# Order and issue of the last convolution step's loads in a fused state-space and feed-forward kernel

## The chip, the cores and the metric

The kernel runs on one core of a Trainium2 chip. The metric is the device time of one execution in microseconds (us). Several executions of a kernel are taken, and their median is compared. One more execution is recorded by the hardware profiler; its span, from the first to the last instruction, is what the profile's views are about. PE is the matrix engine, DVE the vector engine, ACT the scalar engine, POOL and SP the engines that here mainly issue DMAs.

## The reference, cut to what matters

For x of 2048 positions and D = 576 channels, with xn = layernorm(x), the kernel computes

```python
out = x + A(xn) + B(xn)
# A: a long convolution along the positions, one filter per channel
K = einsum("dn,dnl,dn->dl", C, exp(dt*A)**l, dt*B).real     # 576 filters of length 2048
A(u) = irfft(rfft(pad(u)) * rfft(pad(K)))[:2048] + u * Dskip
# B: a feed-forward layer, F = 4608
B(u) = silu(u @ w1) @ w2
```

All of it is in float32.

## The kernel before, in words

**The feed-forward part** is the main line of the program (`ffn`, L231). The positions are cut into 16 tiles j of 128; tiles 0 to 7 are half 0, tiles 8 to 15 half 1, and four tiles make a block. F is cut into 9 chunks c of 4 x 128. The loop runs over `(half, c, b)`, 36 blocks numbered from 0. A block has up products (`up`, L283: x by w1, then silu and a split into a high and a low part, gh and gl) and down products (`down`, L303: by w2, added to the tile's accumulator `acc` by DVE, L320). Products are taken in three passes over high and low parts. A block's steps are u0, d0, d1, d2, d3, u1, u2, u3: its four down products, and the four up products of the block behind it, t = 0 to 3. An up product is 14 matmuls on 512 columns, a down product 24 on 288. The last chunk, c = 8 of half 1, is blocks 34 and 35; its weights are asked for in block 32 (L382: `load_w1` 0, `load_w2` 0 and 1, `load_w1` 2, `load_w2` 2 and 3), and `pins["load"]` is the last load so far. For that chunk the loads with t = 2 and 3 go into the pool `yp` (L243, L268), which takes the place of the pool `kl` of the spectral part.

When half 0 is done, its accumulators are written to `dr0` in DRAM (L323) and the buffers go to half 1. The convolution is added to tiles 0 to 7 later: `dr0` is loaded again in pairs of tiles (`load_r0`, L733, tile `r0`, shown as `r` in the profile), the convolution is added, and the pair is stored to the output by POOL (`store`, L169, issue on L172). Tiles 8 to 15 get theirs in the accumulator, at the head of their last down product (L307 to L309). At the end of the program tiles 8 to 15 are stored by SP, POOL and ACT (L862 to L865).

**The convolution** is a side line (`side`, L805): a transform of the inputs, of the filters, and products of both, written to `d2` in DRAM (`spectral`, L675; 32 stores by POOL, L724). Its last step is `add_conv` (L783): for tile j it takes the tile `ys` (two DMAs of 288 KB on SP, `conv_load`, L776), does 8 small float32 matmuls with the fixed matrix s4 into two PSUM tiles `py` (L793; they show as 16 records, 64*32 rows by columns, 288 columns), and adds both to the destination by DVE (L799). A tile of `ys` takes rows from all 32 stores of d2. There are 8 buffers of ys, 4 of r0 and 3 of `pss`, from which py comes.

**What sets the order.** `weave` (L32) runs the side line between the steps of the main line: a side step with the number `at` is run as soon as `at * 288 <= i + 1`, where i + 1 counts the main line's steps. Block n has the counts 5 + 8n to 12 + 8n (u0 first), so block 32 has 261 to 268, block 33 269 to 276, block 34 277 to 284, and block 35, which has only d0 to d3, 285 to 288. Such a count is called a gate here. The framework then puts each engine's instructions in order itself, by a simulated timeline and by priority (L940: `schedule_with_timeline_sim=True`); an instruction traced earlier has the higher priority, `high_priority` raises it, and `behind(ins)` (L135) keeps what is traced inside it behind `ins` on the same engine. In `add_conv` the first of the matmuls stays behind the last feed-forward matmul traced so far, and the others are of high priority behind the first.

The last step is written out in `tail` (L729). With `tail_at = (0.895, 0.0045, 0.922, 0.005)` the loads are spread over gates from 258 to 273 (L743 to L747), and convolutions 0 to 7 (`last`, L737) over gates from 266 to 276. They are run sorted by these numbers, and `last(j)` first asks for the tile six further on, if that is tile 8 or later; `down` does the same for its own tiles (L308):

```python
        steps, at = [], tail_at[0]
        for j in range(8):
            for f in (conv_load, load_r0)[:2 - j % 2]:
                steps.append((at, f, j))
                at += tail_at[1]
        steps += [(tail_at[2] + j * tail_at[3], last, j) for j in range(8)]
```

Of the kernel before, what the change touches and what calls it, by code (L numbers as in the profile page):

```python
# [11 lines left out]
F32 = mybir.dt.float32  # L12
# [6 lines left out]
P = 128  # L19
# [4 lines left out]
NJ = 16  # L24
NKT = 4
HD = D // 2
# [16 lines left out]
def kernel(  # L43
# [89 lines left out]
    pins = {}  # L133

    def behind(ins):  # L135
        return tc.issue_after(ins) if ins is not None else nullcontext()
# [24 lines left out]
    def load_x(j, pool, tag, engines):  # L161

        t = pool.tile([P, 2, D], F32, tag=tag, name=f"{tag}{j}")
        for ps, v, eng in quarters(xv, engines):
            eng.dma_start(t[ps], v[:, j:j + 2])
        pairs[j] = t
        return t[:, 0, :], t[:, 1, :]

    def store(t, j, engines):  # L169

        for ps, v, eng in quarters(ov, engines):
            eng.dma_start(v[:, j:j + 2] if len(t.shape) > 2 else v[:, j], t[ps])  # L172
# [26 lines left out]
    def phase0(p0, js):  # L199
        j0 = js[0]  # L200
        xs = load_x(j0, accp, "acc", (nc.sync, nc.scalar) if j0 < 4 else (nc.sync,))
        acc.update(zip(js, xs))
        if j0:
            normed(p0, js, xs)
        else:
            for j, xj in zip(js, xs):
                normed(p0, (j,), (xj,))
# [23 lines left out]
    def ffn():  # L231
# [71 lines left out]
        def down(blk, jj):  # L303
            half, c, b = blk
            j = 8 * half + 4 * b + jj
            js = slice(jj * P, (jj + 1) * P)
            if half == 1 and c == NCH - 1:  # L307
                conv_load(j + AHEAD)  # L308
                add_conv(j, acc[j])  # L309
            for h in range(2):  # L310
                hs = slice(h * HD, (h + 1) * HD)
                po = ps2.tile([P, 512], F32, tag="ps2", name="po")
                n = 0
                for t in range(FT):
                    for g, w in ((0, 0), (0, 1), (1, 0)):
                        pins["pe"] = nc.tensor.matmul(po[:, :HD], G[blk, t][g][:, js], W2[half, c, t][w][:, hs],  # L316
                                                      start=n == 0, stop=n == 3 * FT - 1).ins
                        n += 1
                with tc.high_priority():
                    nc.vector.tensor_add(acc[j][:, hs], po[:, :HD], acc[j][:, hs])  # L320
            if half == 0 and c == NCH - 1:
                rows = slice(j * P, (j + 1) * P)
                nc.sync.dma_start(dr0[rows, :], acc[j])  # L323
                if j % 2:
                    acc[7 + j], acc[8 + j] = load_x(7 + j, accp, "acc", (nc.sync,))
# [398 lines left out]
            nc.gpsimd.dma_start(d2.rearrange("(p k) d -> k p d", k=32)[k], yo)  # L724
            yield 1 + (k + 1) / 32

    AHEAD = 6

    def tail():  # L729

        r0s = {}

        def load_r0(j):  # L733
            r0s[j] = yp.tile([P, 2, D], F32, tag="r0", name="r0", bufs=4)
            nc.sync.dma_start(r0s[j], dr0[j * P:(j + 2) * P, :].rearrange("(i p) d -> p i d", p=P))

        def last(j):  # L737
            conv_load(j + AHEAD, 8)
            add_conv(j, r0s[j - j % 2][:, j % 2, :])
            if j % 2:  # L740
                store(r0s[j - 1], j - 1, (nc.gpsimd,))

        steps, at = [], tail_at[0]  # L743
        for j in range(8):
            for f in (conv_load, load_r0)[:2 - j % 2]:
                steps.append((at, f, j))
                at += tail_at[1]  # L747
        steps += [(tail_at[2] + j * tail_at[3], last, j) for j in range(8)]
        for at, f, j in sorted(steps, key=lambda v: v[0]):
            yield at  # L750
            with behind(pins["load"]):
                f(j)

    yss = {}

# [17 lines left out]
                nc.tensor.matmul(dst, st, mv[:, hs], start=n == 0, stop=n == 3 * len(terms) - 1)  # L773
                n += 1

    def conv_load(j, first=0):  # L776
        if first <= j < NJ:
            yss[j] = yp.tile([P, 4, HD], F32, tag="ys", name="ys", bufs=AHEAD + 2)
            for h in range(2):
                nc.sync.dma_start(yss[j][64 * h:64 * h + 64],  # L780
                                  d2[j * 256:(j + 1) * 256, h * HD:(h + 1) * HD].rearrange("(q r) d -> r q d", q=4))

    def add_conv(j, dst):  # L783

        ys = yss.pop(j)
        py = [pss.tile([P, 512], F32, tag="pss", name="py") for _ in range(2)]
        first = pins["pe"]
        for n in range(8):
            q1, q2, h = n // 4, n // 2 % 2, 1 - n % 2
            o = 64 * q1 + 32 * q2  # L790
            rows = slice(64 * h, 64 * h + 64)
            with tc.high_priority() if n else nullcontext(), behind(first):
                mm = nc.tensor.matmul(py[h][o:o + 32, :HD], s4[rows], ys[rows, 2 * q2 + q1],  # L793
                                      start=True, stop=True, tile_position=(64 * h, o), skip_group_check=True)
            if n == 0:
                first = mm.ins
        for h in range(2):
            hs = slice(h * HD, (h + 1) * HD)
            nc.vector.tensor_add(dst[:, hs], py[h][:, :HD], dst[:, hs])  # L799

    def gate_of(i):

        return (FT + i * 2 * FT + 1) / (2 * NCH * 2 * 2 * FT)

    def side():  # L805
        nonlocal s4, kl, yp, pa, tail_at
        marks = (0.13, 0.597, 0.823)
        tail_at = (0.895, 0.0045, 0.922, 0.005)
        with tc.tile_pool(name="pa", bufs=4) as pa:
            for js in ((0, 1), (2, 3), (4, 5), (6, 7)):  # L810
                with behind(pins["xt3"] if js[0] > 2 else None):
                    phase0(pa, js)
                pins[f"xt{js[1]}"], pins[f"xt{js[1]}s"] = pins["xt_v"], pins["xt_s"]
                if js[0] == 2:
                    yield 0
            yield 0
        with tc.tile_pool(name="kf", bufs=1) as kfp:
            for n in ("f", "phi"):
                kf[n] = kfp.tile([P, D], F32, name=n + "T")
            with tc.tile_pool(name="nat", bufs=1) as nat, tc.tile_pool(name="pb", bufs=1) as pb:  # L820
                nt = natural(nat)
                def late(j):

                    xs = load_x(j, pb, "xj", (nc.sync,))
                    yield
                    with behind(pins["gl"]):
                        normed(pb, (j, j + 1), xs)
                    yield

                tiles = chain.from_iterable(late(j) for j in range(8, NJ, 2))  # L830
                for at, todo in ((0.0, nt), (0.0, tiles), (0.004, tiles), (0.005, tiles), (gate_of(0), nt), (0.026, tiles), (0.028, tiles), (0.036, tiles), (0.038, tiles), (gate_of(1), nt), (0.06, tiles), (gate_of(2), nt), (0.09, nt)):
                    yield at
                    with behind(pins["gl"] if at else None):
                        next(todo, None)
            with behind(pins["sd"]):
                nc.gpsimd.dma_start(f1, cf1)
            nc.sync.dma_start(vt, cv)
            with tc.tile_pool(name="up", bufs=1) as up:
                sp = spread(up)
                for n, at in enumerate(kgen()):  # L840
                    if n > 1:
                        next(sp, None)
                    yield marks[0] + at * (marks[1] - marks[0])
                for _ in sp:
                    pass
        s4p = ctx.enter_context(tc.tile_pool(name="s4p", bufs=1))
        s4 = s4p.tile([P, 32], F32, name="s4")
        nc.gpsimd.dma_start(s4, cs4)

        with tc.tile_pool(name="kl", bufs=2) as kl:  # L850
            for at in spectral():
                yield marks[1] + (at - 1) * (marks[2] - marks[1])
        yp = ctx.enter_context(tc.tile_pool(name="yp", bufs=3))
        yield from tail()

    sd = side()
    next(sd)
    fg = ffn()
# [85 lines left out]
```

## Time and profile before

| what | us |
|---|---|
| median of 3 executions | 1133.96 |
| lowest and highest of them | 1133.13, 1138.07 |
| the profiled execution | 1134.37 |
| its span | 1132.6 |
| PE busy in the span | 1108.6 |
| DVE busy | 916.8 |
| ACT busy | 709.3 |

The mean granted clock of PE is 0.997 of full speed. DMA moved 148.56 MB, 131 GB/s over the span. The busy time of an engine says how much of the span it worked, not whether it set the end; for that one reads the chain of work that ended last, the waits of the busiest engine, and the stretches in which it was idle. An issue on SP or POOL is a short entry in that engine's list; the transfer itself lands some microseconds later. In a list in order of time each line has the start, the length, the engine, the line of the kernel, the operation, the tile written and the tiles read, the shape and the count of merged instructions; in brackets stands how long the engine had been idle before, and what ended it.

### The profile page before, as it was taken

The page shows a single profiled execution, that of the slowest core. Times are in us where ns is not written, and L with a number is a line of the kernel's source. Part 1 is how long each engine was busy: PE and PEld are TensorE (multiplying, and loading weights), DVE is VectorE, ACT ScalarE, POOL GpSimd, SP SyncE. Part 2 cuts the span into 40 slices and gives each one's busy share as a digit, 9 for nine tenths or more (in the row PEclk, how much of TensorE's full clock was granted, in tenths as well). Part 3 has the DMA queues.
Part 4 walks back from the last instruction along what each step waited for, and adds up shares of the span by engine and source line. Part 5 has one row for each costly group of instructions (what it writes and reads, how often), then busy time and mean ns, then how long its engine had stood idle before and what let it go on. Part 6 is the DMA issues. An engine that isn't in the chain of part 4 may idle for free.

```text
span 1132.6 us, 22870 instructions
## 1 busy us (share of the span) xinstructions
PE 1108.6 (98%) x9144; PEld 998.8 (88%) x9144; DVE 916.8 (81%) x1545; ACT 709.3 (63%) x1229; POOL 73.0 (6%) x130
## 2 busy tenths in 40 slices
PE   6999999999999999999999999999999999999898
PEld 5988889898898898889989999999999999997776
DVE  6798799999999899999999737777778787773433
ACT  4565366677767676676766636787777787772211
POOL 1100100000000000011000000000000000001110
PEclk9999999999999999999999999999999999999999
DMA  9546431425252415265743263554555454426971
GB/s 277 152 121 168 122 83 60 107 81 128 71 116 84 115 60 129 70 152 168 193 143 93 67 165 115 150 154 134 160 152 159 127 158 141 132 89 170 248 179 56
DMA packets 174971, 148.56 MB, mean 131 GB/s; under 512 B 110944, under 2 KB 141680, under 8 KB 174736
## 3 DMA queue, kind: packets, MB, share of 16 engines
q1 hardware_dynamic: 164768, 112.07, 37.8%
q0 software_dynamic: 9712, 34.14, 9.4%
q8 instruction: 72, 1.18, 0.5%
q10 hardware_dynamic: 384, 0.89, 0.3%
q14 instruction: 35, 0.29, 0.1%
HBM read 102.53 MB, written 44.61 MB: 130 GB/s over the span
## 4 chain that ended last, share of the span: by engine, by line
PE 77%; DMA 7%; DVE 7%; issue 4%; SPq 2%; ACT 2%; POOL 0%; ACTq 0%; DVEq 0%; POOLq 0%
PE po L316 33%; PE ph L291 27%; DMA ys<-d 3%; PE kp L641 3%; PE ph L293 2%; PE ph L292 2%; PE pu L773 2%; PE pk L773 2%; PE pb L773 2%; PE z L656 2%; PE pu L154 1%; SPq L228 1%; DVE st L181 1%; DMA xj<-in_A_u_dram 1%; DVE gl L301 1%
## 5 line engine op out<-in xcount | busy, mean ns | idle before, releaser
L316 PE MATMUL po<-w2h,gh 128*128 128x288 f32 x1152 | 338.6, 298 | 1.0 <-ACT w2h L278 0.9
L316 PE MATMUL po<-w2l,gh 128*128 128x288 f32 x1152 | 339.0, 295 | 0.0
L316 PE MATMUL po<-w2h,gl 128*128 128x288 f32 x1152 | 337.1, 296 | 2.0 <-DVE gl L301 1.8
L316 PEld LDWEIGHTS po<-w2h,gh 128*128 128x128 f32 x1152 | 215.9, 188 | 11.6 <-issue 3.7
L316 PEld LDWEIGHTS po<-w2h,gl 128*128 128x128 f32 x1152 | 216.1, 188 | 4.8 <-DVE gl L301 2.8
L316 PEld LDWEIGHTS po<-w2l,gh 128*128 128x128 f32 x1152 | 217.0, 188 | 3.7
L299 ACT ACTIVATE gf<-ph 128x512 f32<-128x512 f32 (+1 forms) x148 | 86.5, 585 | 126.1 <-PE ph L293 109.3
L320 DVE TENSOR_TENSOR acc<-po,acc 128x288 f32<-128x288 f32 x288 | 127.1, 454 | 46.9 <-PE po L316 45.0
L291 PE MATMUL ph<-xh,w1h 128*128 128x512 f32 (+1 forms) x592 | 163.3, 391 | 1.4 <-ACT xh L124 0.7
L291 PE MATMUL ph<-xl,w1h 128*128 128x512 f32 (+1 forms) x592 | 162.9, 389 | 0.0
L291 PE MATMUL ph<-xh,w1l 128*128 128x512 f32 (+1 forms) x592 | 162.5, 387 | 0.3 <-DVE w1l L261 0.3
L301 DVE TENSOR_TENSOR gl<-gf,gh 128x512 fp32r<-128x512 f32 (+1 forms) x148 | 99.4, 674 | 39.8 <-ACT gh L300 39.0
L291 PEld LDWEIGHTS ph<-xl,w1h 128*128 128x128 f32 x592 | 109.5, 191 | 20.7
L291 PEld LDWEIGHTS ph<-xh,w1l 128*128 128x128 f32 x592 | 108.2, 189 | 21.0 <-DVE w1l L261 0.7
L291 PEld LDWEIGHTS ph<-xh,w1h 128*128 128x128 f32 x592 | 105.7, 190 | 20.3 <-issue 2.3
L300 ACT CAST gh<-gf 128x512 fp32r<-128x512 f32 (+1 forms) x148 | 89.8, 609 | 14.2 <-PE po L316 11.2
L278 ACT CAST w2h<-w2r 128x576 fp32r<-128x576 f32 x72 | 46.9, 672 | 44.8 <-PE po L316 27.9
L600 ACT ACTIVATE c<-th 128x1040 f32<-128x1040 f32 x36 | 38.7, 1074 | 49.3 <-DVE th L599 49.3
L598 ACT ACTIVATE c<-th,magic 128x1040 f32<-128x1040 f32 x36 | 42.0, 1168 | 33.2 <-DVE th L584 17.2
L261 DVE TENSOR_TENSOR w1l<-w1r,w1h 128x640 fp32r<-128x640 f32 x72 | 57.1, 822 | 0.2
L292 PE MATMUL ph<-x,w1h 128*128 128x512 f32 (+1 forms) x148 | 57.1, 386 | 0.0
L293 PE MATMUL ph<-x,w1l 128*128 128x512 f32 (+1 forms) x148 | 57.1, 386 | 0.0
(182 smaller groups left out, 1829.2 us busy)
## 6 DMA issues: line engine op xcount, KB each, us to landing
w2r<-in_B_w_dram SPq DMA_DIRECT2D x72, 288.0 KB, 3.3
w1r<-in_B_w_dram SPq DMA_DIRECT2D x35, 512.0 KB, 4.1
d1u<-u POOLq DMA_DIRECT2D x32, 288.0 KB, 2.7
d1k<-stage SPq DMA_DIRECT2D x18, 512.0 KB, 7.4
ur<-d1u SPq DMA_DIRECT2D x32, 288.0 KB, 4.1
kr<-d1k SPq DMA_DIRECT2D x32, 288.0 KB, 2.8
d<-yo POOLq DMA_DIRECT2D x32, 288.0 KB, 3.6
ys<-d SPq DMA_DIRECT2D x32, 288.0 KB, 12.4
```

Source lines behind the costliest of these rows:

```text
L261: pins["w1l"] = nc.vector.tensor_sub(l1, src, h1).ins
L278: pins["w2h"] = nc.scalar.copy(h2, r2).ins
L291: nc.tensor.matmul(ph, w[:, kt, :], v[:, kt, a:e], start=n + kt == 0, stop=False)
L292: nc.tensor.matmul(ph, h1[:, 4, :], x4[:, a:e], start=False, stop=False)
L293: pins["pe"] = nc.tensor.matmul(ph, l1[:, 4, :], x4[:, a:e], start=False, stop=True).ins
L299: nc.scalar.activation(gf, ph, AF.Silu)
L300: pins["gh"] = nc.scalar.copy(gh, gf).ins
L301: pins["gl"] = nc.vector.tensor_sub(gl, gf, gh).ins
L316: pins["pe"] = nc.tensor.matmul(po[:, :HD], G[blk, t][g][:, js], W2[half, c, t][w][:, hs], start=n == 0, stop=n == 3 * FT - 1).ins
L320: nc.vector.tensor_add(acc[j][:, hs], po[:, :HD], acc[j][:, hs])
L598: nc.scalar.activation(c65, th, AF.Identity, bias=magic)
L773: nc.tensor.matmul(dst, st, mv[:, hs], start=n == 0, stop=n == 3 * len(terms) - 1)
```

## The change

The six-ahead rule is gone. `conv_load` takes no tile any more; each call takes the next of a fixed order, 0 to 3, 8 to 11, 4 to 7, 12 to 15. At gate 263 the first eight loads are traced at once, with r0 pairs 0 and 2 among them, all behind `pins["load"]`, which by then is the last weight load of the last chunk. The other eight are asked for behind a convolution each, so each takes the buffer that this convolution has read. r0 pairs 4 and 6 are loaded behind convolutions 1 and 2. Convolutions 0 to 3 have the gates 269 to 272 and convolutions 4 to 7 the gates 278, 279, 280 and 282 (0.932 and 0.965 of 288 and 0.0036 apart). Convolutions 8 to 15 stay at the heads of their down products.

```diff
--- before.py
+++ after.py
@@ -305,8 +305,8 @@
             j = 8 * half + 4 * b + jj
             js = slice(jj * P, (jj + 1) * P)
             if half == 1 and c == NCH - 1:
-                conv_load(j + AHEAD)
                 add_conv(j, acc[j])
+                conv_load()
             for h in range(2):
                 hs = slice(h * HD, (h + 1) * HD)
                 po = ps2.tile([P, 512], F32, tag="ps2", name="po")
@@ -724,7 +724,8 @@
             nc.gpsimd.dma_start(d2.rearrange("(p k) d -> k p d", k=32)[k], yo)
             yield 1 + (k + 1) / 32
 
-    AHEAD = 6
+
+    order = iter((0, 1, 2, 3, 8, 9, 10, 11, 4, 5, 6, 7, 12, 13, 14, 15))
 
     def tail():
 
@@ -735,21 +736,22 @@
             nc.sync.dma_start(r0s[j], dr0[j * P:(j + 2) * P, :].rearrange("(i p) d -> p i d", p=P))
 
         def last(j):
-            conv_load(j + AHEAD, 8)
             add_conv(j, r0s[j - j % 2][:, j % 2, :])
+            conv_load()
             if j % 2:
                 store(r0s[j - 1], j - 1, (nc.gpsimd,))
 
-        steps, at = [], tail_at[0]
+        yield tail_at[0]
+        with behind(pins["load"]):
+            for j in (0, None, 2, None, None, None, None, None):
+                conv_load()
+                if j is not None:
+                    load_r0(j)
         for j in range(8):
-            for f in (conv_load, load_r0)[:2 - j % 2]:
-                steps.append((at, f, j))
-                at += tail_at[1]
-        steps += [(tail_at[2] + j * tail_at[3], last, j) for j in range(8)]
-        for at, f, j in sorted(steps, key=lambda v: v[0]):
-            yield at
-            with behind(pins["load"]):
-                f(j)
+            if j in (2, 3):
+                load_r0(j * 2)
+            yield tail_at[1 + j // 4] + j % 4 * tail_at[3]
+            last(j)
 
     yss = {}
 
@@ -773,9 +775,11 @@
                 nc.tensor.matmul(dst, st, mv[:, hs], start=n == 0, stop=n == 3 * len(terms) - 1)
                 n += 1
 
-    def conv_load(j, first=0):
-        if first <= j < NJ:
-            yss[j] = yp.tile([P, 4, HD], F32, tag="ys", name="ys", bufs=AHEAD + 2)
+    def conv_load():
+
+        j = next(order, None)
+        if j is not None:
+            yss[j] = yp.tile([P, 4, HD], F32, tag="ys", name="ys", bufs=8)
             for h in range(2):
                 nc.sync.dma_start(yss[j][64 * h:64 * h + 64],
                                   d2[j * 256:(j + 1) * 256, h * HD:(h + 1) * HD].rearrange("(q r) d -> r q d", q=4))
@@ -805,7 +809,7 @@
     def side():
         nonlocal s4, kl, yp, pa, tail_at
         marks = (0.13, 0.597, 0.823)
-        tail_at = (0.895, 0.0045, 0.922, 0.005)
+        tail_at = (0.91, 0.932, 0.965, 0.0036)
         with tc.tile_pool(name="pa", bufs=4) as pa:
             for js in ((0, 1), (2, 3), (4, 5), (6, 7)):
                 with behind(pins["xt3"] if js[0] > 2 else None):
```

## The prediction

> **What bounds the kernel now.** I read the page first, then the busy times in stretches of 20 us, then who waited for whom on PE, and last the lists of PE, SP and POOL in order of time.
>
> ```profile
> span 1132.6 us, 22870 instructions
> PE 1108.6 (98%) x9144; PEld 998.8 (88%) x9144; DVE 916.8 (81%) x1545; ACT 709.3 (63%) x1229; POOL 73.0 (6%) x130
> ```
>
> PE is busy for 98% of the span: only PE time, or idle time of PE, can change the total. So I look for PE's idle time by stretch (columns: stretch, length, then busy time and count of each engine, granted clock, DMA share, GB/s).
>
> ```profile
> 1000.00:1020.00 20.00, 20.00 (x121) 18.16 (x120) 13.40 (x26) 15.23 (x32) 1.08 (x2) 1.00 0.23 67
> 1020.00:1040.00 20.00, 19.00 (x136) 16.68 (x134) 7.62 (x15) 5.06 (x9) 0.54 (x1) 1.00 0.55 144
> 1040.00:1060.00 20.00, 16.69 (x117) 12.93 (x118) 7.75 (x15) 4.26 (x7) 3.91 (x8) 0.91 1.08 252
> 1060.00:1080.00 20.00, 19.38 (x145) 15.37 (x144) 7.96 (x16) 4.84 (x8) 1.93 (x4) 1.00 1.07 261
> 1080.00:1100.00 20.00, 19.16 (x178) 14.77 (x179) 8.15 (x18) 1.85 (x4) 2.90 (x6) 1.00 0.73 176
> ```
>
> From 900 to 1020 PE (first busy number) is full. It has gaps from 1039 to 1081, and there the DMA engines are saturated (share 1.08 and 1.07, 252 and 261 GB/s) and one stretch has a lower granted clock, 0.91. PE's waits from 960 on are a single line (total, times, longest), and its list shows one of them:
>
> ```profile
> PE py L793 <- DMA ys<-d: 5.8, 4, 2.1
> ```
>
> ```profile
> 1043.02 0.39 PE L292 MATMUL ph<-x,w1h 128*128 128x512 f32 x1
> 1043.33 0.69 PE L793 MATMUL py<-ys,s 64*32 64x288 f32 x8
> 1043.95 0.50 PE L293 MATMUL ph<-x,w1l 128*128 128x512 f32 x1
> ...
> 1055.18 0.84 PE L793 MATMUL py<-ys,s 64*32 64x288 f32 x16 [2.08 <-DMA ys<-d]
> 1055.95 0.40 PE L316 MATMUL po<-w2h,gh 128*128 128x288 f32 x1
> ...
> 1056.70 0.44 PE L316 MATMUL po<-w2l,gh 128*128 128x288 f32 x1
> ...
> 1064.04 0.72 PE L793 MATMUL py<-ys,s 64*32 64x288 f32 x16
> 1064.68 0.40 PE L316 MATMUL po<-w2h,gh 128*128 128x288 f32 x1
> ```
>
> All four waits are for tiles of the last convolution step: 0.99 before 1039.97 (tile 1), 1.23 before 1048.90 (tile 2), 2.08 before 1055.18 (tile 3), 1.46 before 1080.85 (tile 7): 5.76 us. Behind the third the down products start 0.240 us apart instead of 0.132 from 1056.46 to 1059.58: 14 of them lose 14 x 0.108 = 1.5 us. Why the tiles are late stands in the lists of POOL and SP:
>
> ```profile
> 1026.79 0.54 POOL L724 DMA_DIRECT2D d<-yo  x1 [7.09 <-ACT yo L723]
> ```
>
> ```profile
> 1029.41 1.28 SPq L780 DMA_DIRECT2D ys<-d  x2
> 1030.74 0.60 SPq L735 DMA_DIRECT2D r<-dr  x1
> 1031.38 1.24 SPq L780 DMA_DIRECT2D ys<-d  x2
> 1032.66 0.61 SPq L246 DMA_DIRECT2D w1r<-in_B_w_dram  x1
> ...
> 1047.25 14.12 SPq L780 DMA_DIRECT2D ys<-d  x8
> 1061.72 0.58 SPq L735 DMA_DIRECT2D r<-dr  x1
> 1063.07 21.04 SPq L780 DMA_DIRECT2D ys<-d  x14
> ```
>
> Every tile needs the whole of d2. The last store to it is issued at 1026.79 and the first load starts at 1029.41. Then 16 tiles, four pairs of r0 and the last weights go through engines that are already full. The step gates give the order of tiles 0, 1, 2, 3, 4, 5, 8, 6, 9, 10, 7: tile 7, due in block 33, stands behind tiles 8 to 10, due in block 34.
>
> **A model of the landings.** I count in units of 288 KB (0.295 MB), half a tile: a tile is 2, a pair of r0 2, a pair's store 2, the last chunk's remaining weights (640 KB in three transfers and two of 288 KB) 4.2. At 252 GB/s a unit takes 1.17 us. Tile 3 landed at 1055.1 with 8 + 4 + 4.2 + 2 = 18.2 units behind 1029.4; tile 7 at 1080.7 with 40.2 (tiles 0 to 10, four pairs, weights, three stores: 22 + 8 + 4.2 + 6). Both fit 1033.4 + 1.17 x units (1054.7 and 1080.4), an estimate from these rows.
>
> **The change, part by part.**
>
> *The places of the convolutions.* Convolutions 0 to 3 move from gates 266 to 270 to gates 269 to 272: behind u0, d0, d1, d2 of block 33 and no longer from block 32's u2 on. An up product takes 3.19 us (14 x 0.2275), a down product 3.17 (24 x 0.132), a convolution in between 0.85 (0.65 plus 0.09 before and 0.11 after). Block 32's u1 ends at 1034.3; u2, u3 and u0 follow, so convolution 0 starts at 1043.9, and 1, 2, 3 4.0 us apart: 1047.9, 1051.9, 1055.9. Then d3, three ups and u0 of block 34, and convolution 8 at 1072.6. Convolution 4 comes behind d0 at 1076.6, 5 and 6 some 4.9 apart, 7 behind u1 at 1094. The same 16 x 16 matmuls, 32 adds and 32 loads remain: no work goes or comes.
>
> *The loads.* Now the 4.2 units of weights go ahead, then tile 0, r0 pair 0, tiles 1, 2, pair 2, tiles 3, 8 to 11. By the model tile 0 lands at 1040.7 (6.2 units), 1 at 1045.3 (10.2), 2 at 1047.7, pair 2 at 1050.0, 3 at 1052.4, or 1054.7 with a store in between. Margins against PE: 3.2, 2.6, 4.2, and 1.2 to 3.5 us for tile 3. As a cross-check without the model: ahead of tiles 2 and 3 stand the same bytes as before, and they landed by 1048.9 and 1055.1, still 3.0 and 0.8 us in time. Tile 11 comes at 24.2 units plus two stores, 1066.4, against some 1087. So the 5.76 us go, because each convolution is 4 to 15 us later in PE's order while its tile isn't. I give back 0.5 for a short wait at tile 1 or 3 (between 0 and 2.1, the longest wait before; nearest to the margins worked out).
>
> *Loads as buffers come free.* Tile 4's load waits on SP for convolution 0's matmuls (1044.6), that of tile 5 for 1's, and so on. Behind these waits on SP stand only other tiles, r0 pairs 4 and 6 and the last stores of the output (1094 before). Tile 4 then is the 30th unit: 1068.7 against 1076.6; pair 4 the 34th: 1073.4 against its add at 1077.5; pair 6 1078 against 1087; tile 7 1080.4 against 1094; tiles 12 to 15, freed by 8, 4, 9 and 5 from 1073 on, are due from some 1101 on. Nothing here is on the path, with 4 us to spare at least.
>
> *The clock.* The slow stretch follows tile 3's wait; with the wait gone I take its 1.5 us off as well. [...]
>
> *Splits.* A convolution in one go costs 0.85, in two halves (x8 each 0.62 plus 0.20) 1.64. Three are split: 1 (1039.97 and 1043.33), 7 (1080.85 and 1082.13) and 14 (1119.44 and 1120.91): 0.79 each. Where the new order will split is not to be seen. Bounds: all three gone, -2.4; three more, +2.4. Tiles 1 and 7 are the ones that were late, 14 keeps its place: I take one gone, -0.8. Convolutions 4 and 9 (5 and 10, 6 and 11) become neighbours with three PSUM buffers for two each: at worst a wait for one 0.46 us add, three times, +1.4; at best a shared change-over, -0.6; down products can stand in between, so I take 0.
>
> *POOL and the end.* The stores of pairs 4 and 6 go from 1070 and 1083 to some 1083 and 1096; POOL's next issues stood at 1094.6, 1102.7 and 1120.2, each 1 to 2 us. What follows PE's end (1128.3 to 1132.6: add and last store) is as it was.
>
> **The sum.** The profiled execution took 1134.37 us, its span 1132.6 plus 1.77 around it. 1134.37 - 5.76 - 1.5 - 0.8 + 0.5 = 1126.8. The median shown, 1133.96, is 0.41 lower; I carry that over: **1126.4**.
>
> **The rivals.**
>
> - *The clock term stays.* The slow stretch has another cause: 1126.4 + 1.5 = 1127.9. For it: the gap of 1.46 us before 1080.85 brought no slow stretch; against: it is the only one from 900 to 1120 and starts 1.3 us after the longest wait. Chance 0.08.
> - *The first tiles are still waited for.* The order on PE comes from a simulated timeline, and before, it put convolution 0 inside u2. If convolutions 0 to 3 stand one product (3.2 us) ahead of where I put them, 3 comes at 1052.7, its tile at 1055.1: 2.4 us of wait and the clock's 1.5 again: with the 0.5 in my sum, 1126.4 + 3.4 = 1129.8. For it speak the thin margins at tiles 1 and 3. Chance 0.17.
> - *Slower: r0 pair 4 comes too late.* It is now the 34th unit behind 1029.4, and its add stands on DVE ahead of gl, which feeds the down products; before, DVE sat idle 5.36 us for pair 2 (to 1051.82). If the units take 1.65 us each, pair 4 lands at 1085.8, and some 7.6 us of wait cancel the gain; from 1.83 us (1092, 13.5 us of wait) the kernel is 0.5% slower, about 1140. Against it: tile 7 before came at (1080.7 - 1029.4) / 40.2 = 1.28 us a unit. Chance 0.07.
> - *It doesn't do what it says.* The schedule puts the convolutions back where the gaps are, and waits change places only: 1134, give or take 2. Chance 0.06.
>
> **How the numbers follow.** My forecast has the remaining 0.62; with the bounds of the splits and neighbours it spans 1123.8 (all splits gone, no wait, shared change-overs) to 1129. About 0.5%, 5.7 us, is what a measurement of this kernel can tell from no change: faster means under 1128.3. Nearly all of my forecast, most of the clock case and a little of the third lie there: 0.66. Slower (over 1139.6): 0.07, the r0 case. The rest, 0.27, lies within. The range must reach over the second rival: 1123.8 to 1132; outside are the slower case, the last and a thin edge.
>
> **What would show it.** In the changed profile SP should list w1r and two w2r ahead of the first ys at about 1029.4; PE's waits should hold no py <- DMA ys above 1 us; convolution 0 at about 1044 and 8 at about 1073; the granted clock 1.00 from 1040 to 1060 and PE there above 19.5 us of 20; PE's last product at about 1120. A DVE wait on DMA r for pair 4 would point to the slower case; a slow stretch without a wait ahead of it, to the first.

## The result, and the profile after

The changed kernel takes 1126.96 us (median of 5, 1126.24 to 1127.91), the kernel before 1133.96 us (median of 5, 1131.79 to 1138.07). The ratio is 0.993, with a 95% interval from 0.9904 to 0.9956. The forecast was 1126.4 us.

The page of the changed kernel has the same work on PE, in a shorter span:

```profile
span 1124.6 us, 22864 instructions
PE 1106.4 (98%) x9144; PEld 995.8 (89%) x9144; DVE 917.1 (82%) x1545; ACT 709.1 (63%) x1229; POOL 72.9 (6%) x130
```

The busy times by stretch (length, then busy time and count of PE, PEld, DVE, ACT, POOL, then granted clock, DMA share, GB/s):

```profile
1020.00:1040.00 20.00, 20.00 (x123) 18.27 (x122) 5.62 (x10) 4.85 (x9) 0.54 (x1) 1.00 0.62 166
1040.00:1060.00 20.00, 20.00 (x167) 15.48 (x166) 10.89 (x23) 5.06 (x9) 3.91 (x8) 1.00 1.07 270
1060.00:1080.00 20.00, 20.00 (x139) 15.38 (x138) 6.89 (x13) 5.45 (x9) 0.00 (x0) 1.00 0.76 206
1080.00:1100.00 20.00, 20.00 (x170) 14.28 (x167) 8.10 (x18) 1.22 (x2) 5.81 (x12) 1.00 0.69 186
```

PE is now full in every stretch, the clock is 1.00, and the list of PE's waits from 960 us on has no line at all. The DMA engines are as full as before in the second stretch (1.07 against 1.08) and less so in the third (0.76 against 1.07). SP's list shows what goes first now; ahead of it stands the last line of POOL's list for `d2`, the store that the tiles need:

```profile
1024.39 0.54 POOL L724 DMA_DIRECT2D d<-yo  x1 [7.09 <-ACT yo L723]
```

```profile
1026.99 0.38 SPq L246 DMA_DIRECT2D w1r<-in_B_w_dram  x1
...
1028.61 1.06 SPq L269 DMA_DIRECT2D w2r<-in_B_w_dram  x2
1029.71 1.28 SPq L784 DMA_DIRECT2D ys<-d  x2
1031.04 0.60 SPq L736 DMA_DIRECT2D r<-dr  x1
...
1036.31 16.58 SPq L784 DMA_DIRECT2D ys<-d  x10
1053.43 1.54 SPq L736 DMA_DIRECT2D r<-dr  x2
1055.08 26.36 SPq L784 DMA_DIRECT2D ys<-d  x14
```

One thing has to be taken out before the two profiles are compared. The last store to d2 starts at 1024.39 here and at 1026.79 before, although nothing ahead of it was changed: 2.40 of the 8.0 us between the spans arose earlier. So for the last step I take the stretch from the start of that store to the end of the last add on DVE, and call it the **last step**:

```profile
1120.30 0.46 DVE L320 TENSOR_TENSOR acc<-po,acc 128x288 f32<-128x288 f32 x1 [1.14 <-PE po L316]
```

It ends at 1120.76, 96.37 us behind the store. The same line of the kernel before:

```profile
1128.30 0.46 DVE L320 TENSOR_TENSOR acc<-po,acc 128x288 f32<-128x288 f32 x1 [1.14 <-PE po L316]
```

There the last step took 1128.76 - 1026.79 = 101.97 us. The gain in this pair of profiles is 5.60 us.

PE's list also holds something that the forecast did not have. There are 22 groups of small py matmuls in place of 19, because seven convolutions are split: 1, 2, 4, 9, 10, 11 and 14 (before: 1, 7 and 14). Three of the groups, with down products in between:

```profile
1076.22 0.69 PE L797 MATMUL py<-ys,s 64*32 64x288 f32 x8
...
1077.43 0.72 PE L797 MATMUL py<-ys,s 64*32 64x288 f32 x16
...
1079.46 0.69 PE L797 MATMUL py<-ys,s 64*32 64x288 f32 x8
```

The middle one is no whole convolution: DVE adds one half of it to `r` (1078.19, the second half of convolution 4) and the other to `acc` (1078.57, the first half of convolution 9). So seven splits make six groups more than sixteen whole convolutions would. The expectations below call these six groups six split convolutions.

### The profile page after: what moved, and what is told of

The parts are those of the page before. It is cut to its first block, busy times and chain, and to the rows that moved or that the text cites. A ratio compares the mean times of both kernels' runs of the same rounds, so it can differ in the third digit from the quotient of the medians.

```text
span 1124.6 us, 22864 instructions
## 1 busy us (share of the span) xinstructions
PE 1106.4 (98%) x9144; PEld 995.8 (89%) x9144; DVE 917.1 (82%) x1545; ACT 709.1 (63%) x1229; POOL 72.9 (6%) x130
## 4 chain that ended last, share of the span: by engine, by line
PE 86%; DVE 8%; DMA 3%; ACT 1%; issue 1%; SPq 1%; POOL 0%; ACTq 0%; DVEq 0%
PE po L316 36%; PE ph L291 30%; PE kp L641 3%; PE ph L292 2%; PE ph L293 2%; PE pu L775 2%; PE pb L775 2%; PE pk L775 2%; PE z L656 2%; PE py L797 1%; PE pu L154 1%; DMA xj<-in_A_u_dram 1%; DVE acc L320 1%; DVE gl L301 1%; PE pu L155 1%
## 5 line engine op out<-in xcount | busy, mean ns | idle before, releaser
L320 DVE TENSOR_TENSOR acc<-po,acc 128x288 f32<-128x288 f32 x288 | 126.6, 451 | 38.0 <-PE po L316 35.7
```

## The experiments

Each of the ten was timed beside the kernel before, and a ratio is against those executions of the kernel before. Their medians were 1134.3 us for the first four rows, 1134.23 us for the next four and 1132.78 us for the last two; a ratio isn't exactly the ratio of the medians. The first four pull the change apart; the next four test the weights' place and the price of the split convolutions; the last two look for where the splits come from.

| kernel | median us | ratio (95% interval) | last step us |
|---|---|---|---|
| before, once more | 1135.24 | 1.0001 (0.9983 to 1.0018) | 104.57 |
| places only | 1130.45 | 0.9964 (0.9944 to 0.9984) | 102.71 |
| loads only | 1137.22 | 1.0021 (1.0005 to 1.0036) | 106.24 |
| change, tiles loaded in natural order | 1127.85 | 0.9943 (0.9921 to 0.9965) | 96.36 |
| change, convolutions 4 to 7 apart | 1126.16 | 0.9937 (0.9918 to 0.9957) | 95.64 |
| change, loads ahead of the weights | 1137.44 | 1.0039 (1.0023 to 1.0055) | 105.83 |
| change, convolutions whole | 1123.27 | 0.9913 (0.989 to 0.9935) | 93.02 |
| change, apart and whole | 1122.55 | 0.9899 (0.988 to 0.9918) | 92.09 |
| change, four PSUM buffers for py | 1149.35 | 1.0154 (1.0128 to 1.018) | not compared |
| all three | 1150.58 | 1.0152 (1.0131 to 1.0173) | not compared |

**The kernel before, once more.** No edit.

> The kernel before once more, unchanged. It asks how much of the profiles' difference is chance: in the two profiles the last store to d2, ahead of anything the change touches, is already 2.4 us apart (1026.79 and 1024.39). If the waits in the last step belong to the kernel, this profile has them again: four waits of py for ys, 5 to 6.5 us in all, and a slow stretch of the clock behind the longest. If the slow stretch has a cause of its own, it is absent here or stands elsewhere. Time: 1134, give or take 2, ratio 1.00.

The waits came again, 6.8 us in four, and the last step took 104.57 us, 2.6 more than in the first profile. The slow stretch stands elsewhere. PE's list of this run:

```profile
1078.90 0.69 PE L793 MATMUL py<-ys,s 64*32 64x288 f32 x8 [3.41 <-DMA ys<-d]
1079.52 0.99 PE L291 MATMUL ph<-xh,w1h 128*128 128x512 f32 x2
...
1082.58 1.91 PE L291 MATMUL ph<-xl,w1h 128*128 128x512 f32 x4
1084.28 1.91 PE L291 MATMUL ph<-xh,w1l 128*128 128x512 f32 x4
```

Four up matmuls take 1.70 us here (1082.58 to 1084.28) against 0.92 ahead of the wait (1073.96 to 1074.88), behind the wait for tile 7, which is now the longest at 3.41 us; the granted clock from 1080 to 1100 is 0.83. Tile 3's wait of 2.04 us had no slow stretch behind it, while its 2.08 us in the first profile had one. So in these two profiles the slow stretch goes with a wait, 2.08 us in one and 3.41 us in the other, and not with a place in the program; but of the two waits of about 2 us one has it and the other doesn't.

**Places only.** The loads stay as in the kernel before; convolutions 0 to 7 move to gates 269 to 276.

```diff
-        tail_at = (0.895, 0.0045, 0.922, 0.005)
+        tail_at = (0.895, 0.0045, 0.932, 0.0036)
```

> Only the places: the loads as in the kernel before (order, spreading, the first ones ahead of the weights), but convolutions 0 to 7 at gates 269 to 276 in place of 266 to 276. PE's order up to convolution 3 is that of the changed kernel. My theory (the waits go because the convolutions stand later): no wait at tiles 1 to 3 and no slow stretch, but tile 7 stands behind tiles 8 and 9 in SP's list and comes at about 1077 for a convolution due at about 1073, a wait of 2 to 4 us; five split convolutions against three cost 1.6. Sum: 1134 - 7.3 + 3 + 1.6 = 1131. The rival (the loads' order and weights ahead do it, not the places): the waits stay, and the splits come on top, 1134 to 1136.

Measured 1130.45. The waits at tiles 1 to 3 are gone; PE's only wait from 960 us on is tile 7's, and the granted clock from 1060 to 1080 is 0.88:

```profile
PE py L793 <- DMA ys<-d: 4.4, 1, 4.4
```

So later places alone do cure the first tiles, with all loads as they were, and tile 7 pays for standing behind tiles 8 and 9 in SP's list. Its load landed some 52 us behind the last store (PE went on at 1076.14, the store was at 1023.94), where the landing model had 50.

**Loads only.** Eight loads at once behind the last weights and the others as buffers come free, in the natural order, with the convolutions at their old gates. The edit is to the changed kernel:

```diff
-    order = iter((0, 1, 2, 3, 8, 9, 10, 11, 4, 5, 6, 7, 12, 13, 14, 15))
+    order = iter(range(16))
...
-        tail_at = (0.91, 0.932, 0.965, 0.0036)
+        tail_at = (0.91, 0.922, 0.942, 0.005)
```

> Only the loads: eight at once behind the last weights, the others as buffers come free, in the natural order 0 to 15; convolutions 0 to 7 at their old gates 266 to 276. The rival (the loads do it): the waits go, 1134 - 7.3 = 1127. My theory: tiles 0 to 3 land as late as before or later, since the weights now go ahead, and convolutions 0 to 3 still stand early: waits of 1 to 3 us each at tiles 0 to 3, 4 to 5 us in all, perhaps the slow stretch again; 1131 to 1134.

Measured 1137.22, 0.2% slower than before and worse than my theory said. The waits for tiles are smaller than expected (1.9 us in two; the 1.3 us put down to `r` stand before convolution 0, whose matmuls read only ys and s4, so they are probably a third one), but a larger one came where I had none. PE's waits, then DVE's list around the largest, then PE's:

```profile
PE py L797 <- DVE r L803: 5.8, 1, 5.8
PE py L797 <- DMA ys<-d: 1.9, 2, 1.3
PE py L797 <- DMA r<-dr: 1.3, 1, 1.3
```

```profile
1061.77 0.46 DVE L320 TENSOR_TENSOR acc<-po,acc 128x288 f32<-128x288 f32 x1 [1.14 <-PE po L316]
1071.60 0.82 DVE L803 TENSOR_TENSOR r<-py,r 128x288 f32<-128x288 f32 x2 [9.38 <-DMA r<-dr]
1072.34 0.45 DVE L320 TENSOR_TENSOR acc<-po,acc 128x288 f32<-128x288 f32 x1
```

```profile
1065.68 0.67 PE L797 MATMUL py<-ys,s 64*32 64x288 f32 x2
1072.11 1.21 PE L797 MATMUL py<-ys,s 64*32 64x288 f32 x14 [5.76 <-DVE r L803]
```

DVE sat idle 9.38 us for r0 pair 4, then did everything that stood behind that add at once. Convolution 4 held its two PSUM buffers until that add, so convolution 5 had only the third one and stopped behind the first of its eight matmuls (2 of 16 records). This is the mechanism of my slower rival, in a kernel in which pair 4's load stands behind two tiles that wait for free buffers while convolution 4 keeps its early place. In the changed kernel convolution 4 starts 51.8 us behind the last store in place of 35.7, and DVE has no wait on the r0 loads.

**The change with tiles in natural order.** One line of the change is undone.

```diff
-    order = iter((0, 1, 2, 3, 8, 9, 10, 11, 4, 5, 6, 7, 12, 13, 14, 15))
+    order = iter(range(16))
```

> The changed kernel with one part undone: the loads come in the natural order 0 to 15 (so tiles 4 to 7 ahead of 8 to 11). PE's order of instructions is the same as in the changed kernel, with six split convolutions. By my model of landings tile 8 is then the 30th unit behind the first load, 1069 on the clock of the profile of before, for a convolution due at 1074 to 1076: no wait, ratio to the changed kernel 1.00 within 0.001, 1127. The rival (the order of the tiles matters): tiles 8 to 11 are waited for, 2 us or more in PE's waits, and the time is 1129 or above.

Measured 1127.85, no wait on PE, and a last step of 96.36 us against 96.37. PE's order of instructions is the same, so this is the cleanest pair here: the order of the tiles, which gives the change its name, is worth nothing once the places are late. It makes a second pair with the run before it: loads only and this kernel have the same loads in the same order and differ in the places of convolutions 0 to 7 alone, and the last step falls from 106.24 to 96.36 us, the ratio from 1.0021 to 0.9943. Its profiled span is 1127.5 us, 2.9 more than the changed kernel's, and all of that lies ahead of the last step.

**Convolutions 4 to 7 apart.**

```diff
-        tail_at = (0.91, 0.932, 0.965, 0.0036)
+        tail_at = (0.91, 0.932, 0.9755, 0.0035)
```

> The changed kernel with convolutions 4 to 7 at gates 281 to 284 in place of 278, 279, 280 and 282: behind d3, u1, u2, u3 of block 34, so no longer beside convolutions 9 to 11. PE's order now has five split convolutions in place of six. I measure from the last store to d2 to the last add (before: 102.0 and 104.6 us in two profiles, changed kernel 96.4). By my price of a split, 0.79, this falls to 95.6 and the time to 1126; no wait of py. The rival (neighbouring convolutions cost by waits for PSUM buffers rather than by splits): nothing to gain, 96.4.

The last step took 95.64 us, 0.73 less than the changed kernel's 96.37, for one group of py fewer, 21 in place of 22 (0.79 expected). The medians, 1126.16 against 1126.96, were not taken side by side and the ranges of the executions overlap; it is the profile that tells these two apart.

**Loads ahead of the weights.**

```diff
-        tail_at = (0.91, 0.932, 0.965, 0.0036)
+        tail_at = (0.895, 0.932, 0.965, 0.0036)
```

> The changed kernel with its first eight loads and two r0 pairs traced at gate 258, ahead of the last chunk's weights, so that w1r and w2r of t = 2 and 3 land behind some 20 units. By the landing model w1r lands 35 us behind the last store to d2; u2 of block 33 wants it, split, at about 36.5. My theory (there is room for either order): a wait of 0 to 1.5 us of PE for w1h or w1l, no wait of py, five splits; 95.6 to 97 from the last store to the last add, 1126 to 1127.5. The rival (putting the weights ahead is what pays): PE waits 2 us or more for the weights, 98 or above.

Measured 1137.44 and a last step of 105.83: the rival was right. PE had one wait, for an accumulator add; DVE's and ACT's lists show what it stood behind:

```profile
PE po L316 <- DVE acc L320: 8.6, 1, 8.6
```

```profile
1060.40 1.35 ACT L259 CAST w1h<-w1r 128x640 fp32r<-128x640 f32 x2 [15.43 <-DMA w1r<-in_B_w_dram]
```

```profile
1047.83 0.46 DVE L803 TENSOR_TENSOR r<-py,r 128x288 f32<-128x288 f32 x1 [0.75 <-PE py L797]
1061.16 0.83 DVE L261 TENSOR_TENSOR w1l<-w1r,w1h 128x640 fp32r<-128x640 f32 x1 [12.87 <-ACT w1h L259]
1061.90 0.45 DVE L320 TENSOR_TENSOR acc<-po,acc 128x288 f32<-128x288 f32 x1
```

The landing was as the model had it: ACT's split starts 36.0 us behind the last store (1060.40 - 1024.42), 35 was worked out. My error was the due time. I took the moment at which PE's u2 wants the weights; but in DVE's list the split of these weights stands ahead of the accumulator adds of d1 of block 33, and there it is due at 1048.3, 12 us sooner.

**Convolutions whole.** Each product's first matmul is held behind the convolution traced ahead of it.

```diff
+                    with behind(pins.pop("conv", None)):
                         nc.tensor.matmul(ph, w[:, kt, :], v[:, kt, a:e], start=n + kt == 0, stop=False)
...
+                        with behind(pins.pop("conv", None)):
                             pins["pe"] = nc.tensor.matmul(po[:, :HD], G[blk, t][g][:, js], W2[half, c, t][w][:, hs],
...
                 first = mm.ins
+        pins["conv"] = mm.ins
```

> The changed kernel with each feed-forward product held behind the convolution traced ahead of it, so that convolutions run nearly whole: 14 groups of py on PE in place of 22. My theory (a split costs 0.79 because each half takes 0.62 against 0.65 for the whole, plus 0.2 for the change-over): 10 single groups at 0.85, the four larger ones 1.2, 0.8 and twice 1.5 plus some 0.6 of waiting for a PSUM buffer each, 14.7 against 18.3 in all: 3.6 us less, 92.8 from the last store to the last add, 1123.4. The rival (splits are harmless, since products that run ahead of a convolution cover the waits for gl and for PSUM): no gain, or 1 to 3 us of new waits of po for gl or py for DVE, 96 to 99.

Measured 1123.27 and a last step of 93.02 us, where 92.8 was worked out. PE's list of the changed kernel, with a split convolution, and of this kind of kernel (here the next one), with a whole one:

```profile
1045.84 0.69 PE L797 MATMUL py<-ys,s 64*32 64x288 f32 x8
1046.46 0.40 PE L316 MATMUL po<-w2h,gl 128*128 128x288 f32 x1
...
1047.05 0.69 PE L797 MATMUL py<-ys,s 64*32 64x288 f32 x8
1047.67 0.40 PE L316 MATMUL po<-w2h,gl 128*128 128x288 f32 x1
```

```profile
1045.95 0.72 PE L799 MATMUL py<-ys,s 64*32 64x288 f32 x16
1046.60 0.40 PE L318 MATMUL po<-w2h,gh 128*128 128x288 f32 x1
```

Half a convolution, 8 records, holds PE 0.62 us (1045.84 to 1046.46), a whole one, 16 records, 0.65 (1045.95 to 1046.60). The two halves lie in different rows of the array (64 * h in L797), and in one go the second half adds 0.03 us. Pulled apart, the two take 1.24.

**Apart and whole.** The two edits above together.

> Both: convolutions 4 to 7 at gates 281 to 284, and each product held behind the convolution ahead of it; 15 groups of py, one of them a double. My theory: 14 x 0.85 + 2.1 = 14.0 against 18.3, so 4.3 us less than the changed kernel: 92.1 from the last store to the last add, 1122.7. The rival (splits harmless): 96 or more.

Measured 1122.55, a last step of 92.09 us, as worked out (92.1), and no wait on PE from 1000 us on. This version beats both kernels: 0.9899 of the kernel before (0.988 to 0.9918), and all its executions (1120.49 to 1123.99) lie below those of the changed kernel (1126.24 to 1127.91), though the two were not timed side by side.

**Four PSUM buffers for py.** One buffer is taken from the down products.

```diff
-    ps2 = ctx.enter_context(tc.tile_pool(name="ps2", bufs=3, space=PSUM))
-    pss = ctx.enter_context(tc.tile_pool(name="pss", bufs=3, space=PSUM))
+    ps2 = ctx.enter_context(tc.tile_pool(name="ps2", bufs=2, space=PSUM))
+    pss = ctx.enter_context(tc.tile_pool(name="pss", bufs=4, space=PSUM))
```

> The changed kernel with four PSUM buffers for py (pss) and two for po (ps2), in place of three and three. In PE's order no convolution is split any more: 13 groups, three of them doubles. My theory (a split comes from the third buffer that the next convolution must wait for): 10 x 0.85 + 3 x 1.5 = 13.0 against 18.3 us, 5.3 less in the last step, if po does with two buffers; time 1121.7. The rival (two buffers are too few for po): PE waits of po for DVE acc all over the kernel, and a time above the changed kernel's 1127.

In PE's order no convolution is split, which agrees with splits that come from the third buffer; as the edit took a buffer from po too, it doesn't prove it. And the kernel is 1.5% slower than before, 1149.35 us: the rival was right on the whole kernel. PE's waits for the accumulator adds stand over all of it (there is no such line in the kernel before):

```profile
PE po L316 <- DVE acc L320: 10.0, 16, 2.5
```

**All three** (apart, whole, four buffers).

> Convolutions 4 to 7 behind d3, u1, u2, u3 of block 34, each product held behind the convolution ahead of it, and four PSUM buffers for py with two for po. 15 groups of py, the double one without a wait: 14 x 0.85 + 1.5 = 13.4 against 18.3, 4.9 us less than the changed kernel, 1122. If po with two buffers waits for DVE, it is slower than the same kernel with three, 1122.55.

Measured 1150.58, as slow; a fourth buffer for py isn't worth one of the down products'.

## Why the prediction was right, and which term was not

**The bound and the waits: right.** The four waits of py for ys and the slow clock behind them went completely. They were not all that the last step could lose: without splits it is another 4.3 us shorter (92.09 against 96.37). I had given back 0.5 us for a short wait; there was none.

**The cause: right, and the experiments say more.** I put the gain down to the convolutions standing later in PE's order. Places alone remove the waits at tiles 1 to 3; the loads alone are 0.2% slower than before; and with the new loads in natural order the places take 9.9 us off the last step (106.24 to 96.36). The places of convolutions 0 to 3 are not enough: in places only, with convolutions 4 to 7 at gates 273 to 276, tile 7 is late by 4.4 us. It came 52 us behind the last store, and in the changed kernel convolution 7 starts 71.7 us behind it; so the later places should cure tile 7 with the old loads too, but no run has the old loads with all the new places. Of the loads' parts, the order of the tiles is worth nothing (96.36 against 96.37 us). The weights' place is no gain over the kernel before, in which only two tiles and a pair stood ahead of them and PE waited for no weights. It is a condition of asking for eight tiles at once: with these ahead of the weights the last step takes 105.83 us against 96.37. I had seen that the weights go first, not that DVE needs it.

**The landing model: right within 2 us** wherever it could be read: 35 against 36.0 us behind the last store for w1r with the loads ahead, 50 against 52 for tile 7 with places only. The weights started at 1026.99, which is 1029.39 on the clock of the profile before; 1029.4 was forecast. PE came later than I put it: convolution 0 at 18.6 us behind the last store (17.1 forecast) and convolution 8 at 49.0 (45.8), so the convolutions had 1.5 to 3.2 us more than I gave them.

**The clock: right in the main.** The changed kernel has no slow stretch, and the stretch moved with the longest wait in the repeated profile, against the rival that it has another cause. From 960 us on, five waits of PE have a slow stretch behind them: 2.08 us (kernel before), 3.41 (before, once more), 4.35 (places only), 5.76 (loads only) and 8.59 (loads ahead of the weights). None of the others, 0.28 to 2.04 us long, has one. The longest without and the shortest with one are 0.04 us apart, in two profiles of the same kernel; why the wait of 2.08 us was followed by a slow stretch and the one of 2.04 us was not stays open.

**The splits: wrong.** The step "I take one gone, -0.8" failed. PE has 22 groups of py in place of 19; my sum had 18. Three more groups at 0.79 are +2.4 us, my upper bound, and 3.2 us worse than the sum had it. Four of the seven split convolutions (4, 9, 10, 11) are among the neighbours whose term I had put at 0. The price itself held: 0.73 less for one group fewer, and 92.09 measured for 92.1 worked out without splits.

**Why the time still fits.** In the profile that the sum was made from, 5.76 + 1.5 - 2.4 leaves 4.9 of the 5.60 us measured; 0.7 I can't assign. The measured 5.60 is 2 us less than my 7.6. On the other side the kernel before can lose more in another execution: in its second profile 6.8 us of waits and, by the excess of the slow matmuls, some 3.3 of clock, so 104.57 - 96.37 = 8.2 us. The medians, 7.0 us apart, lie between the two. So a term 3.2 too good and a profile that happened to be a good one nearly cancelled. That is luck: 1126.4 was closer than its working deserved.

**The rivals.** The first tiles were not waited for; their margins were wider than I had them. The r0 rival did not happen in the changed kernel, but its mechanism did with loads only: a late pair cost 9.4 us of DVE and 5.8 of PE. The rival that waits only change places was refuted by the empty list of waits. Two figures of the working don't come out of the numbers beside them, and nothing hangs on them: the bounds of the splits and the neighbours reach 1126.4 + 3.2 + 1.4 = 1131.0, not 1129; and pair 4 at 1085.8 or 1092 against an add at 1077.5 is 8.3 or 14.5 us of wait, not 7.6 or 13.5.

## What to carry to other kernels

A load that is late on a full set of DMA engines can be cured by moving its consumer, where other work can go ahead of it (places only: no wait at tiles 1 to 3, at a DMA share of 1.07 from 1040 to 1060): count the units that stand ahead of it, and put the consumer behind that much other work. For each operand that moves back in the queue, look for its due time in the lists of all engines, not only of the bounding one; an add or a split that waits on DVE holds up what stands behind it (9.38 us for a pair of r0, 12.87 for the weights). And when small matmuls of which half takes nearly as long as the whole (0.62 against 0.65 us here) are placed between large ones, count the groups in the new order: each one that comes apart has a price (0.73 us here for one group).

## What the runs showed of the hardware that was not expected

The kernel before is not steady in its last step, 101.97 and 104.57 us in two profiles, because its waits differ (5.8 and 6.8 us) and a wait had a slow clock behind it (2.08 us) or not (2.04 us); the changed kernel and its variant in natural order, in which PE never waits there, gave 96.37 and 96.36. Two profiles of each kind are few.

The slow stretches were of different length: 3.4 us in the first profile (1056.46 to 1059.82), some 6.9 in the second (1079.52 to 1086.42).

The profiles' spans differ by up to 3.5 us ahead of anything that was changed (last store to d2 between 1023.94 and 1027.42 in ten profiles with the same work up to there). All of it arises before the first of the 32 stores to d2: from the first to the last each of the ten takes 322.94 to 322.96 us (before: 703.84 to 1026.79; changed kernel: 701.44 to 1024.39). A difference of that size between two spans says nothing before it is traced to its stretch.
